# 400 pairs of row maxima beside the projections, and one exponential for two heads

## The chip, the cores and the metric

The kernel runs on one core of a Trainium2 chip, whose engines work side by side: TensorE (PE in the profile, its weight loads PEld), VectorE (DVE), ScalarE (ACT), GpSimd (POOL), and SyncE (SP), whose queue issues the transfers. The metric is the device time of one execution in microseconds (us).

## What is computed

Two transformer layers with the same weights over 2048 tokens of width 640. Each layer is

```python
x = x + attention(layernorm(x)) @ wo        # 32 heads of 20
h = relu(layernorm(x) @ w1 + b1)
x = x + (h * h) @ w2 + b2                   # 1536 hidden
```

where attention is `softmax(q k^T / sqrt(20)) v` over all 2048 keys, for every head. Most matrices are held as two parts, a high one and the rest, and multiplied in three products (high by high, high by rest, rest by high).

## The kernel before

**Heads and blocks.** Four heads form a group (8 groups); a block `t` is one group against one quarter `qb` of the queries (512 of them): 32 blocks a layer. In a group, head `2 * p + par` lies on the upper or lower 64 partitions by `par`, so a score product takes 60 rows there, or 62 with two more that carry the negated row maximum.

**Maxima.** The softmax subtracts each query's true maximum, which must be known before a block's scores are made. It is found by a product of its own the other way round: 128 queries by 512 keys (`by_queries`, L463), reduced along the keys on VectorE into a small tile `mx`. For each block there are 2 pairs of heads x 4 groups of 128 queries x 4 key quarters `c`, so 32 *pairs* (a pair: both `par`), 1024 a layer. They are found in three ways:

- `smax` (L475): one head, one bank, one reduction of 512; used inside attention.
- `smax_two` (L484): a pair on two banks, one reduction of 1024; used beside the projections.
- *doubles*: for two neighbouring key quarters at once. From the difference of the keys (`kd`, made beside the projections and stored in `d_kd`) `step_two` makes a pair of products and ScalarE's relu of them (L495); `both_two` makes the products with the first quarter, and VectorE adds the relu and takes the maximum (L505, with a short read of the accumulator). So one double stands for two plain pairs, with the same number of products and half the passes over them on VectorE.

**The projection stage** (`qkv`): 40 units of 15 products make q and k (L308), 16 of 30 make v (L355). `between` counts products, and at every `PACE` of them calls `some`, which puts maxima between: the end of a double begun in the last call, one plain pair, and the start of a double; three uses of two-bank pieces. These come in turn from banks 0 to 5 (`ps_q`). The lists `PLAIN` and `DOUBLE` say which blocks are ready at which unit; a plain item is `(group, qb, c)`, a double `(group, qb, "d")` for quarters 0 and 1, `"e"` for 2 and 3. After the doubles the rest is plain, three pairs per 11 products. `tiles` asks for the keys and queries of an item and of the one after it when the item begins.

**Attention** (`attention`): a written order of letters is walked, `a` and `b` a score and its exponential for the even or odd head of a pair (L560, L567), `m` and `n` one maximum for an even or odd head, `V` the weighted sum of a key tile of 128 keys (L572, four heads beside each other in bank 7, single precision in two passes). Each string holds eight key tiles; its key in `ORDERS` is the number of maxima pairs in it, which `pairs` chooses by what is due. Scores use banks 0 to 3 in turn (`ps_st`), maxima 4 to 6. Pairs already done beside the projections are left out of the list. At a block's end ScalarE copies the sums out of bank 7 (L585).

All instructions keep the order in which the program issues them, on each engine; semaphores alone tie the engines.

Of the kernel before, what the change touches and what calls it, by code (L numbers as in the profile page):

```python
# [16 lines left out]
P = 128  # L17
# [22 lines left out]
def tile_layers(  # L40
# [52 lines left out]
    ps_st = Ring(0, 1, 2, 3)  # L93
# [359 lines left out]
    def maxima(t):  # L453
        if t not in mx_t:
            mx_t[t] = small.tile([P, 4, 4, 4], F32, tag="mx", bufs=14, name=name("mx"))
            if t in PARTLY:
                nc.vector.memset(mx_t[t], LEAST)
        return mx_t[t]
# [92 lines left out]
    def score(t, kt, h, es):  # L551

        p, par = divmod(h, 2)
        if p not in es:
            es[p] = weights[len(e_n) % len(weights)]
            e_n.append(t)
        dst = ps_st("st")
        b = 64 * par
        assert t in done
        nc.tensor.matmul(  # L560
            dst,
            k_t[t // NQB, kt // 4][b : b + 62, p, (kt % 4) * P : (kt % 4 + 1) * P],
            q_t[t][b : b + 62, p, :],
            start=True,
            stop=True,
        )
        nc.scalar.activation(es[p][:, par, :], dst, AF.Exp, scale=SCALE)  # L567
# [72 lines left out]
    def prep_job():  # L640
# [7 lines left out]
        if jobs:  # L648
# [11 lines left out]
        ([], [(1, qb, c) for qb in (1, 2, 3) for c in (2, 3)]  # L660
         + [(2, qb, c) for qb in range(3) for c in range(NQB)]),
    ]
    DOUBLE = [
# [4 lines left out]
         [(1, 3, "d"), (1, 0, "e")]),  # L668
# [6 lines left out]
    PACE = 8.2  # L675
# [3 lines left out]
    def qkv(first, x_src, rest):  # L679
# [5 lines left out]
        state = {"pace": 0, "n": 0}  # L685
        early, late, later_rows = {}, {}, []
        coming = [y for x in DOUBLE for h in x for y in h if y[2] == "d"]
# [34 lines left out]
        def tiles(x):  # L722
            g, qb, c = x
            for c in [c] if c in range(4) else [c, 2 * "de".index(c)]:
                if (g, c) not in k_t:
                    if c in range(4):
                        load_k(g, c, g > 1)
                    else:
                        load_kd(g, c)
            if g * NQB + qb not in q_t:  # L730
                load_q(g * NQB + qb)

        def end_group(x):
            g, qb, c = x
            t = g * NQB + qb
            rest = groups + double + [w[0] for w in work + twos] + [w[0][0] for w in begun]
            if t == 0:
                left[t] -= 1 if c in range(4) else 2
                if left[t] == 0:
# [7 lines left out]
            for y in [y for y in k_t if y[0] == g < 2 and y not in use]:  # L747
                del k_t[y]
# [22 lines left out]
        def some():  # L771


            while later_rows:
                mrows_load(later_rows.pop())
            if not (begun or double or twos):
                for _ in range(3):
                    one()
                return
            if begun:  # L780
                w, r = begun.pop()
                (g, qb, x), p, sub = w
                t = g * NQB + qb
                both_two(t, p, sub, x, r)
                c = 2 * "de".index(x)
                done.update([(t, p, sub, c), (t, p, sub, c + 1)])
                if (p, sub) == PAIRS[-1]:
                    end_group(w[0])
            one()
            w = following(double, twos)  # L790
            if w:
                (g, qb, x), p, sub = w
                begun.append((w, step_two(g * NQB + qb, p, sub, x)))
            else:
# [12 lines left out]
        for n, (tb, pos) in enumerate(UNITS):  # L807
# [5 lines left out]
            if 1 < n < NQB * FIRST + 2:  # L813
# [8 lines left out]
                if step == 3:  # L822
                    double.extend(DOUBLE[b][0] + DOUBLE[b][1])
# [6 lines left out]
        for tt in range(NKT):  # L830
            later(v_unit(tt, lambda: between(0.65)))
# [6 lines left out]
            if tt == 12:  # L838
# [3 lines left out]
                load_q(1)  # L842
        w_v.drop()
# [3 lines left out]
        for y in [y for y in k_t if y[0] == 1]:  # L847
            del k_t[y]
        assert 0 in done

# [8 lines left out]
        12: "naambbmVanmbambVbmannabVnabnmabVabnmbanVbbmnanaVbmmbaanVbmbmnaaV",  # L859
    }  # L860

    def attention(first, x_src, first_rows):
# [27 lines left out]
        def begin(i):  # L890
# [14 lines left out]
            if t == 1 and u % 4 == 1:  # L905
                load_k(3, u // 4, True)
# [15 lines left out]
        def op(o):  # L922
            if o in "ab":
# [8 lines left out]
                score(i // NKT, i % NKT, 2 * p + par, es_of.setdefault(i, {}))  # L932
# [40 lines left out]
        def pairs():  # L973
# [7 lines left out]
            n = min(max(round(state["debt"]), 12), 16)  # L981
# [3 lines left out]
        for o in "abab":  # L985
# [226 lines left out]
```

## Time and profile before

| | us |
|---|---|
| time, median of 3 (lowest, highest) | 3765.41 (3762.61, 3766.22) |
| the profiled execution | 3764.07 |
| its span in the profile | 3762.3 |
| projection stage, layer one | up to 373 |
| attention, layer one | 373 to 1464 |
| attention, layer two | 2247 to 3337 |

A group line of the profile names source line, engine, operation, the tile written and those read, the shape and the count; then the engine's busy time in us, the mean ns of one, and the idle time just before these instructions with what ended it. Instructions of one engine overlap, so the busy time divided by the count is less than the mean. A line of the timeline gives the start and length in us of neighbouring instructions of one kind, with their count; its length runs to the end of the last. A line of the windows gives the stretch, its length, and busy time (count) of PE, PEld, DVE, ACT and POOL, then TensorE's granted clock, the share of the transfer engines' time, and GB/s.

### The profile page before, as it was taken

What the parts mean: (1) busy time and instruction counts of PE and PEld (TensorE: products, weight loads), DVE (VectorE), ACT (ScalarE), POOL (GpSimd) and SP (SyncE); (2) the same over time, 40 slices, a digit from 0 to 9 for tenths busy, and PEclk for the clock granted to TensorE, in tenths of its full rate; (3) what the DMA queues carried; (4) which work ended last, traced back from release to release, by engine and by line L of the source; (5) the groups of instructions that cost most, each with busy time, mean ns of one, the idle gap of its engine ahead of it and who ended that gap; (6) DMA issues with size and microseconds to landing.
All of it is one profiled execution on the core that took longest, in us unless ns stands there. A gap on an engine that the chain in (4) does not pass through costs nothing.

```text
span 3762.3 us, 64260 instructions
## 1 busy us (share of the span) xinstructions
PE 3704.9 (98%) x23572; PEld 2127.4 (57%) x23572; DVE 2757.8 (73%) x4726; ACT 2573.2 (68%) x4951; POOL 830.4 (22%) x921
## 2 busy tenths in 40 slices
PE   6999999999999999999999999999999999999999
PEld 4667344444444445989876774444444444368998
DVE  7788888888888882444457878888888888814443
ACT  2454999999999995121224449999999999941221
POOL 6540234321122211111154201211221112101110
PEclk9999999999999999999999999999999999999999
DMA  7563454432212125611255443222222111365111
GB/s 224 182 206 133 130 174 143 146 81 67 64 49 57 44 91 188 230 43 43 95 171 179 160 142 82 77 67 64 70 73 55 54 54 43 98 213 195 43 46 40
DMA packets 258282, 405.87 MB, mean 108 GB/s; under 512 B 67828, under 2 KB 114676, under 8 KB 257968
## 3 DMA queue, kind: packets, MB, share of 16 engines
q1 hardware_dynamic: 257424, 400.06, 33.9%
q8 instruction: 186, 3.05, 0.3%
q10 hardware_dynamic: 544, 1.71, 0.2%
q14 instruction: 128, 1.05, 0.1%
HBM read 264.82 MB, written 136.81 MB: 107 GB/s over the span
## 4 chain that ended last, share of the span: by engine, by line
PE 93%; DMA 2%; DVE 2%; POOL 1%; ACT 1%; SPq 0%; issue 0%; ACTq 0%; DVEq 0%; POOLq 0%
PE banks L572 27%; PE banks L297 20%; PE banks L560 20%; PE banks L463 15%; PE banks L308 6%; PE banks L355 3%; DMA k<-d_qk 1%; DMA q<-d_qk 0%; SPq L76 0%; PE banks L1042 0%; DMA d_qk<-ev 0%; DVE h L268 0%; DVE r L1066 0%; POOL xnT L282 0%; DVE mx L484 0%; DVE bst L255 0%
## 5 line engine op out<-in xcount | busy, mean ns | idle before, releaser
L567 ACT ACTIVATE e<-banks 128x512 f32<-128x512 f32 x4096 | 2110.8, 612 | 52.6 <-PE banks L560 2.2
L475 DVE TENSOR_REDUCE mx<-banks 128x1 f32<-128x512 f32 x2928 | 1841.5, 685 | 218.9 <-PE banks L463 137.5
L560 PE MATMUL banks<-q,k 62*128 62x512 f32 x4096 | 1162.7, 435 | 2.7 <-DVE mx L484 2.2
L463 PE MATMUL banks<-k,q 60*128 60x512 f32 x3744 | 1153.7, 436 | 10.9 <-DMA q<-d_qk 10.1
L572 PE MATMUL banks<-e,vg 128*32 128x512 f32 x8192 | 1093.0, 605 | 0.0
L560 PEld LDWEIGHTS banks<-q,k 62*128 62x128 f32 x4096 | 600.6, 185 | 709.7 <-ACT e L567 668.7
L463 PEld LDWEIGHTS banks<-k,q 60*128 60x128 f32 x3744 | 537.2, 185 | 331.8 <-DVE mx L475 204.0
L495 ACT ACTIVATE rl<-banks 128x512 f32<-128x512 f32 x352 | 191.6, 596 | 255.7 <-PE banks L463 255.5
L572 PEld LDWEIGHTS banks<-e,vg 128*32 128x32 f32 x8192 | 161.6, 108 | 354.6 <-issue 327.6
L297 PE MATMUL banks<-w,h 128*128 128x320 f32 x2304 | 352.6, 311 | 2.9 <-DVE h L268 2.7
L297 PEld LDWEIGHTS banks<-w,h 128*128 128x128 f32 x2304 | 340.6, 188 | 12.4 <-DVE h L268 6.9
L297 PE MATMUL banks<-xnT,w 128*128 128x512 f32 x1440 | 331.8, 391 | 0.0
L1065 ACT ACTIVATE r<-banks,b_t 128x512 f32<-128x512 f32 x96 | 66.1, 689 | 380.8 <-PE banks L297 379.2
L308 PE MATMUL banks<-xnT,wqk 128*128 128x512 f32 x1200 | 324.2, 414 | 1.6 <-POOL wqk L282 1.6
L505 DVE CUSTOM_DVE_ANT_0 rl<-banks,rl 128x512 f32<-128x512 f32 x352 | 229.2, 689 | 121.3 <-PE banks L463 116.2
L297 PEld LDWEIGHTS banks<-xnT,w 128*128 128x128 f32 x1440 | 270.7, 189 | 55.6
L484 DVE TENSOR_REDUCE mx<-banks 128x2 f32<-128x1024 f32 x232 | 279.6, 1221 | 24.9 <-PE banks L463 24.3
L308 PEld LDWEIGHTS banks<-xnT,wqk 128*128 128x128 f32 x1200 | 220.1, 193 | 87.2 <-issue 43.4
L279 POOL CAST mr<-nt 128x32 fp32r<-128x32 f32 x64 | 13.5, 211 | 966.2 <-DVE nt L531 966.2
L616 POOL TENSOR_TENSOR few<-few,minus_t 128x16 f32<-128x16 f32 x62 | 179.9, 2901 | 199.0 <-DMA few<-d_s 197.1
L1085 DVE TENSOR_TENSOR x<-banks,x 128x320 f32<-128x320 f32 x128 | 62.8, 491 | 200.7 <-PE banks L297 191.6
L627 POOL TENSOR_TENSOR o<-o 128x512 f32<-128x512 f32 x62 | 79.6, 1285 | 560.2 <-DMA o<-d_r 276.3
(73 smaller groups left out, 1991.6 us busy)
## 6 DMA issues: line engine op xcount, KB each, us to landing
q<-d_qk SPq DMA_DIRECT2D x756, 80.0 KB
d_qk<-ev SPq DMA_DIRECT2D x80, 512.0 KB
k<-d_qk SPq DMA_DIRECT2D x468, 80.0 KB
x<-d_x SPq DMA_DIRECT2D x96, 320.0 KB
d_o<-ot SPq DMA_DIRECT2D x248, 80.0 KB
ot<-d_o SPq DMA_DIRECT2D x38, 512.0 KB
d_v<-v SPq DMA_DIRECT2D x32, 512.0 KB
vg<-d_v SPq DMA_DIRECT2D x32, 512.0 KB
```

Source lines behind the costliest of these rows:

```text
L297: nc.tensor.matmul(dst, a, b, start=(n == 0), stop=(n == last))
L308: nc.tensor.matmul(dst, w_qk.piece(pos * 10 + hw * KD + k), xt_[tb][k][:, hx, :], start=(n == 0), stop=(n == 3 * KD - 1),)
L355: nc.tensor.matmul(dst[:, :HALF], xt_[tb][k][:, hx, i * P : (i + 1) * P], w_v.piece(k * 4 + hw * 2 + hf), start=(j == 0), stop=(j == 3 * K ...
L463: nc.tensor.matmul(dst, q_t[t][b : b + 60, p, sub * P : (sub + 1) * P], k_t[t // NQB, c][b : b + 60, p, :], start=True, stop=True,)
L475: nc.vector.tensor_reduce(maxima(t)[:, 2 * p + par, sub, c : c + 1], dst, axis=AX.X, op=ALU.max)
L484: nc.vector.tensor_reduce(maxima(t)[:, 2 * p : 2 * p + 2, sub, c], dst, axis=AX.X, op=ALU.max)
L495: nc.scalar.activation(res[par], dst[:, par, :], AF.Relu)
L505: nc.vector.tensor_tensor_reduce(out=r[par], in0=dst[:, par, :], in1=r[par], scale=1.0, scalar=LEAST, op0=ALU.add, op1=ALU.max, accum_out= ...
L560: nc.tensor.matmul(dst, k_t[t // NQB, kt // 4][b : b + 62, p, (kt % 4) * P : (kt % 4 + 1) * P], q_t[t][b : b + 62, p, :], start=True, stop ...
L567: nc.scalar.activation(es[p][:, par, :], dst, AF.Exp, scale=SCALE)
L572: nc.tensor.matmul(acc[32 * h : 32 * h + 32, :], v_t[t // NQB, kt // 8][:, kt % 8, 32 * h : 32 * h + 32], es[p][:, par, :], start=(kt == 0 ...
L616: nc.gpsimd.tensor_tensor(few, few, minus_t, op=ALU.pow)
```

## The change

It has two parts.

In the projection stage doubles are found for the first three groups, but for the first two key quarters of the first block of groups 0 and 1, which stay plain as before: 176 doubles a layer for 88. Together with the plain pairs 400 of the 1024 pairs lie there, 292 before; the last 16 belong to group 3. Once all doubles are ready (`few` is false), `some` ends all doubles that were begun and fills three places with starts of new ones, at most two, so that calls alternate between two ends and one start, and one end and two starts; the pace is then 5.4 products instead of 8.2. Keys of group 2 are loaded for the doubles alone and again in attention, those of group 3 are loaded during the v units and kept, and `mx` has 16 buffers for 14.

In attention the letter `A` stands for both heads of a pair: two products into two neighbouring banks and one exponential over 1024 elements. The order strings may now hold ten pairs per eight key tiles. The strings for 12 and more stay in the source; the built program uses those of 10 and 11.

```diff
-    ps_st = Ring(0, 1, 2, 3)
+        def two(self):
+            self.n += 2
+            b = self.order[(self.n - 1) % len(self.order)]
+            return banks[:, b : b + 2, :]
+
+    ps_st = Ring(3, 0, 1, 2)
...
-    def score(t, kt, h, es):
+    def score(t, kt, h, dst):
...
+    def soft_two(t, kt, p, es):
+
+        e = weights_for(t, p, es)
+        dst = ps_st.two()
+        for par in range(2):
+            score(t, kt, 2 * p + par, dst[:, par, :])
+        nc.scalar.activation(e, dst, AF.Exp, scale=SCALE)
...
-        ([], [(1, qb, c) for qb in (1, 2, 3) for c in (2, 3)]
-         + [(2, qb, c) for qb in range(3) for c in range(NQB)]),
+        ([], []),
     ]
+    LAST = [(3, qb, c) for qb in range(2) for c in range(NQB)]
...
         ([(0, 3, "d"), (0, 3, "e"), (0, 2, "e"), (0, 1, "e"), (0, 0, "e")],
-         [(1, 3, "d"), (1, 0, "e")]),
+         [(1, 3, "d")] + [(1, qb, "e") for qb in range(NQB)]
+         + [(2, qb, x) for qb in range(NQB) for x in "de"]),
...
-    PACE = 8.2
+    PACE = 5.4
...
-            if not (begun or double or twos):
-                for _ in range(3):
-                    one()
-                return
-            if begun:
-                w, r = begun.pop()
-                (g, qb, x), p, sub = w
+            room = 3
+            while begun:
+                (x, p, sub), r = begun.pop(0)
+                g, qb, h = x
                 t = g * NQB + qb
-                both_two(t, p, sub, x, r)
...
+                both_two(t, p, sub, h, r)
...
+                room -= 1
+            if state["few"]:
+                one()
+                room -= 1
+            for _ in range(min(room, 1 if state["few"] and (groups or work) else 2)):
+                w = following(double, twos)
+                if w:
+                    (g, qb, x), p, sub = w
+                    begun.append((w, step_two(g * NQB + qb, p, sub, x)))
+                    room -= 1
+            for _ in range(room):
                 one()
...
-            pace = PACE if double or twos or begun else 11
+            pace = (8.2 if state["few"] else PACE) if double or twos or begun else 11
...
                 if step == 3:
+                    state["few"] = b < 3
...
+            if tt == 1:
+                groups.extend(LAST)
...
+            if tt in (13, 14):
+                for c in range(2 * tt - 26, 2 * tt - 24):
+                    if (3, c) not in k_t:
+                        load_k(3, c, True)
...
+        11: "AnAmnVAnmAVnAmmAVAnmnAVAnmAVmAnmAVAnmAVAmnnAV",
+        10: "AnmAVAnmmAVAmnAVAmmnAVAnmAVAnmnAVAnmAVAnmnAV",
...
-                for h in (0, 1, 2, 3) if g else (0, 1, 2):
+                for h in (0, 1, 2, 3) if g else (0, 1):
...
-                load_k(3, u // 4, True)
+                load_k(2, u // 4, True)
...
+            if o == "A":
+                i, p = divmod(st_n[0], 2)
...
+                soft_two(i // NKT, i % NKT, p, es_of.setdefault(i, {}))
...
-            n = min(max(round(state["debt"]), 12), 16)
+            n = min(max(round(state["debt"]), 10), 16)
...
-        for o in "abab":
+        for o in "AA":
```

More of the change, by code (lines that the diff above doesn't have):

```diff
@@ L454, in maxima @@
         if t not in mx_t:
[L455 removed]
+            mx_t[t] = small.tile([P, 4, 4, 4], F32, tag="mx", bufs=16, name=name("mx"))
             if t in PARTLY:
@@ L566, in score, with weights_for, soft_one @@
         )
-        nc.scalar.activation(es[p][:, par, :], dst, AF.Exp, scale=SCALE)
+    def weights_for(t, p, es):
+        if p not in es:
+            es[p] = weights[len(e_n) % len(weights)]
+            e_n.append(t)
+        return es[p]
+    def soft_one(t, kt, h, es):
+        p, par = divmod(h, 2)
+        e = weights_for(t, p, es)
+        dst = ps_st("st")
+        score(t, kt, h, dst)
+        nc.scalar.activation(e[:, par, :], dst, AF.Exp, scale=SCALE)
+    def soft_two(t, kt, p, es):
+        e = weights_for(t, p, es)
+        dst = ps_st.two()
+        for par in range(2):
+            score(t, kt, 2 * p + par, dst[:, par, :])
+        nc.scalar.activation(e, dst, AF.Exp, scale=SCALE)
     def pv(acc, t, kt, es, heads=(3, 2, 1, 0)):
@@ L684, in qkv @@
         done.clear()
-        state = {"pace": 0, "n": 0}
+        state = {"pace": 0, "n": 0, "few": True}
         early, late, later_rows = {}, {}, []
-        coming = [y for x in DOUBLE for h in x for y in h if y[2] == "d"]
+        coming = [y for x in DOUBLE for h in x for y in h if y[2] == "d" and y[0] < 2]
         def at(when, n, f):
@@ L746, in end_group @@
             use |= {(h, 2 * "de".index(y)) for h, y in use if y not in range(4)}
-            for y in [y for y in k_t if y[0] == g < 2 and y not in use]:
+            for y in [y for y in k_t if y[0] == g < 3 and y not in use]:
                 del k_t[y]
@@ L846, in qkv @@
         load_v(0, 1)
-        for y in [y for y in k_t if y[0] == 1]:
+        for y in [y for y in k_t if y[0] in (1, 2)]:
             del k_t[y]
@@ L922, in op @@
         def op(o):
-            if o in "ab":
+            if o == "A":
+                i, p = divmod(st_n[0], 2)
+                assert st_n[0] == st_n[1]
+                if i >= last:
+                    return
+                st_n[:] = [st_n[0] + 1] * 2
+                if i > state["begun"]:
+                    state["begun"] = i
+                    begin(i)
+                soft_two(i // NKT, i % NKT, p, es_of.setdefault(i, {}))
+            elif o in "ab":
                 par = "ab".index(o)
```

19 lines of the change are left out of this document (5 added, 14 removed).

## The prediction

> **What bounds the kernel now.** I read the engines and the chain of waits first, then the busy time by stage, then single stretches of the timeline.
>
> ```profile
> PE 3704.9 (98%) x23572; PEld 2127.4 (57%) x23572; DVE 2757.8 (73%) x4726; ACT 2573.2 (68%) x4951; POOL 830.4 (22%) x921
> ...
> PE 93%; DMA 2%; DVE 2%; POOL 1%; ACT 1%; SPq 0%; issue 0%; ACTq 0%; DVEq 0%; POOLq 0%
> PE banks L572 27%; PE banks L297 20%; PE banks L560 20%; PE banks L463 15%; PE banks L308 6%; PE banks L355 3%; DMA k<-d_qk 1%; DMA q<-d_qk 0%; SPq L76 0%; PE banks L1042 0%; DMA d_qk<-ev 0%; DVE h L268 0%; DVE r L1066 0%; POOL xnT L282 0%; DVE mx L484 0%; DVE bst L255 0%
> ```
>
> TensorE carries 93% of the chain: weighted sums (L572), scores (L560), maxima (L463). A busy TensorE need not be a full one, so two stages are looked at closely (windows in us; each busy time with its count).
>
> ```profile
> 30.00:375.00 345.00, 329.04 (x1691) 231.79 (x1689) 266.52 (x517) 145.77 (x278) 133.01 (x161) 0.98 0.55 186
> 2281.00:3270.00 989.00, 989.00 (x6960) 398.30 (x6956) 883.94 (x1447) 966.17 (x1885) 188.62 (x172) 1.00 0.24 66
> ```
>
> The first is the projection stage of layer one, the second 29 attention blocks of layer two: 1885 ScalarE instructions are 29 x (64 exponentials + 1 copy). One block is 989 / 29 = 34.10, one key tile 34.10 / 16 = 2.131 us. TensorE's share of one tile:
>
> ```profile
> 805.35 0.50 PE L560 MATMUL banks<-q,k 62*128 62x512 f32 x1
> 805.35 0.73 PE L463 MATMUL banks<-k,q 60*128 60x512 f32 x2
> 805.69 0.71 PE L560 MATMUL banks<-q,k 62*128 62x512 f32 x3
> 806.16 0.40 PE L463 MATMUL banks<-k,q 60*128 60x512 f32 x1
> 806.49 1.07 PE L572 MATMUL banks<-e,vg 128*32 128x512 f32 x8
> 807.48 0.50 PE L560 MATMUL banks<-q,k 62*128 62x512 f32 x1
> ```
>
> Seven products of 60 or 62 rows start between 805.35 and 806.16. Even heads use the array's lower half of rows, odd heads the upper, and two of different halves start together. So the seven make four **slots**; from the second (805.69) to the fourth (806.16) is 0.47, or 0.235 us a slot. First to second is 0.34, last slot to weighted sum 0.33, that sum 0.99; with two slots of 0.235, 2.13 us. The sum of starts equals the tile: TensorE bounds attention. An odd number of maxima wastes half a slot.
>
> ScalarE comes close behind:
>
> ```profile
> L567 ACT ACTIVATE e<-banks 128x512 f32<-128x512 f32 x4096 | 2110.8, 612 | 52.6 <-PE banks L560 2.2
> 806.38 1.57 ACT L567 ACTIVATE e<-banks 128x512 f32<-128x512 f32 x3
> ```
>
> Three exponentials back to back take 1.57 and the last lasts 0.61, so they start (1.57 - 0.61) / 2 = 0.48 us apart. Four need 1.92 of the 2.131.
>
> **Attention after the change.** The order of the built kernel holds per layer 268 tiles with three maxima, 222 with two and 22 with none; before it is 488 with three and 24 with none. A three-tile keeps four slots; a two-tile has three, hence 2.131 - 0.235 = 1.896. That is 222 x 0.235 = **52 us less** per layer, if nothing else becomes late.
>
> The exponential of 1024 elements isn't in the trace. Above, it starts two at 0.48 each, 0.96; below, it saves the fixed part. The elements' price comes from two copies:
>
> ```profile
> L274 ACT COPY r<-banks 128x512 f32<-128x512 f32 x88 | 51.4, 589 | 88.6 <-PE banks L308 41.4 <-PE banks L385 40.3 <-POOL kd L279 4.0
> L364 ACT COPY v<-banks 128x320 f32<-128x320 f32 x64 | 27.5, 429 | 45.3 <-PE banks L355 41.8 <-DMA k<-d_qk 2.9
> ```
>
> (589 - 429) / 192 = 0.83 ns an element, 0.43 us for 512 more: 0.48 + 0.43 = 0.91 us. I take 0.91, as the rate is that of the same engine and bank. Two tiles (one of each kind) last 4.03 and need four: 3.64, at worst 3.84. Either hides behind TensorE. (The Trainium skill, "ScalarE: Activation LUTs", section on what ACT_TABLE_LOAD costs, gives 186 ns + 0.833 ns per element and an overlap of 93 ns: 1039 ns, one every 0.95, an estimate that leaves the sum as it is. Its 612 ns for 512 elements is the row's 612; the overlap here is 0.13.)
>
> The ring is coarser: a pair of banks is written again one tile later, when its whole exponential is done. In a two-tile the first pair starts at 0, its exponential 0.5 later (0.50 for the product in the rows above) and the second at 0.54 + 0.91 = 1.45, done near 2.5. The next tile, a three-tile, writes that pair at 1.90 + 0.34 + 2 x 0.235 = 2.71. Slack 0.2 us: no wait. The copy of a finished block (as long as L274's, 0.6) goes between two exponentials and costs up to 0.2 where it falls behind a two-tile: 16 x 0.2 = 3 us. Tiles without maxima were bound by ScalarE:
>
> ```profile
> 1445.43 1.07 PE L572 MATMUL banks<-e,vg 128*32 128x512 f32 x8
> 1446.43 1.03 PE L560 MATMUL banks<-q,k 62*128 62x512 f32 x4
> 1447.39 1.07 PE L572 MATMUL banks<-e,vg 128*32 128x512 f32 x8
> 1448.39 1.18 PE L560 MATMUL banks<-q,k 62*128 62x512 f32 x4
> 1449.50 0.64 PE L572 MATMUL banks<-e,vg 128*32 128x512 f32 x4
> ```
>
> Two of them take 1449.50 - 1445.43, 2.03 each; after, two exponentials, some 1.85: 22 x 0.18 = 4. Attention: -52 - 4 + 3 = **-53 us a layer**.
>
> **The projection stage after the change.** The 108 pairs come back here. Products for maxima stand in groups of three slots between projection products; in the built order the groups rise from 100 to 136 a layer (64 to 85 between the q and k units, 36 to 51 between the v units). What a group costs:
>
> ```profile
> 188.63 0.39 PE L308 MATMUL banks<-xnT,wqk 128*128 128x512 f32 x1
> 188.95 0.73 PE L463 MATMUL banks<-k,q 60*128 60x512 f32 x4
> 189.52 0.40 PE L463 MATMUL banks<-kd,q 60*128 60x512 f32 x2
> 189.84 2.12 PE L308 MATMUL banks<-xnT,wqk 128*128 128x512 f32 x8
> 191.89 0.74 PE L463 MATMUL banks<-k,q 60*128 60x512 f32 x4
> 190.41 1.32 PE L308 MATMUL banks<-xnT,wqk 128*128 128x512 f32 x5
> 266.80 0.74 PE L463 MATMUL banks<-k,q 60*128 60x512 f32 x4
> 267.37 0.39 PE L463 MATMUL banks<-kd,q 60*128 60x512 f32 x2
> 267.70 2.02 PE L355 MATMUL banks<-wv,xnT 128*128 128x320 f32 x12
> 269.65 0.51 PE L463 MATMUL banks<-k,q 60*128 60x512 f32 x2
> 268.10 1.18 PE L355 MATMUL banks<-wv,xnT 128*128 128x320 f32 x7
> ```
>
> Five projection products take 1.32 with a last one of 0.39: 0.23 each (0.147 for v, from seven in 1.18 with a last of 0.31). A group with eight lasts 191.89 - 188.95 = 2.94; less 8 x 0.2325, 1.08 us. With twelve v products 2.85 - 12 x 0.147 = 1.09. So 36 groups add 36 x 1.085 = **39 us a layer**. Three bare slots would be 0.70 and 25 us; the rest is the change between full and half arrays (188.63 to 188.95 going in, 189.52 to 189.84 coming out, 0.32 each). (The Trainium skill, "TensorEngine Tiling (Array Packing)", Key Properties, says that changing the tiling mode drains TensorE. It speaks against this change, and the rows agree: by slots alone 25, with the drain 39.)
>
> Now what the quicker pace meets. A "double" is a product with the key difference, two relus on ScalarE, a second product and two VectorE reductions that add and take the maximum. Before, a group held one double's end, one plain pair, one double's start, with 8.2 products between; after, it alternates, 5.4 apart: group A ends two doubles and starts one, group B ends one and starts two. Each group goes once round the three bank pairs. VectorE's pace:
>
> ```profile
> 189.58 0.69 DVE L505 CUSTOM_DVE_ANT_0 rl<-banks,rl 128x512 f32<-128x512 f32 x1 [0.48 <-issue]
> 190.20 0.08 DVE L505 DVE_READ_ACCUMULATOR2_ANT mx<- 128x1 f32 x1
> 190.20 0.69 DVE L505 CUSTOM_DVE_ANT_0 rl<-banks,rl 128x512 f32<-128x512 f32 x1
> 190.81 0.08 DVE L505 DVE_READ_ACCUMULATOR2_ANT mx<- 128x1 f32 x1
> 190.81 1.22 DVE L484 TENSOR_REDUCE mx<-banks 128x2 f32<-128x1024 f32 x1
> ```
>
> A reduction starts 189.58 - 188.95 = 0.63 after its group, the next ones 0.61 apart. A and B hold six, 3.7 us, against some 4.65 for two groups on TensorE (one is 5.4 x 0.2325 + 1.08 = 2.34, beside v 8.3 x 0.147 + 1.09 = 2.31), so VectorE is not the bound in sum. But A's four end at 0.63 + 3 x 0.61 + 0.69 = 3.15. The last reads the second bank pair, and B's second slot writes it, at 2.33 + 0.34 = 2.67 after A's start. TensorE stands 0.48 and the release besides; from product to reduction that hand-over takes 0.63 - 0.50 = 0.13, so between 0.48 and 0.61: I take 0.55. The projection products queue behind it; nothing hides that. (Before, the reduction of that pair begins 190.81 - 188.95 = 1.86 in and ends at 3.08; the next group's second slot comes at 2.94 + 0.34 = 3.28.) The next A comes at 4.65 + 0.55 = 5.2 and its third slot, 0.57 in, at 5.77. It writes where B's last relus read:
>
> ```profile
> 189.95 1.09 ACT L495 ACTIVATE rl<-banks 128x512 f32<-128x512 f32 x2 [1.79 <-PE banks L463]
> ```
>
> A relu starts 189.95 - 189.52 = 0.43 after its product, the next 0.49 later, and lasts 0.6. B's four, from its second slot at 3.22, end at 3.22 + 0.43 + 3 x 0.49 + 0.6 = 5.72: no wait, but no slack; a copy of 0.45 in between could make one. The built order has 54 groups of kind B a layer: 54 x 0.55 = **30 us a layer**; bounds 0 and, with such a copy in each cycle, 54.
>
> Not charged: eight more clears of maxima on VectorE, which is idle for 78 of the 345 us, and the moved loads of keys. Loads are asked for one set of eight doubles ahead. That was 8 x 2.94 = 23.5 us and is now 5.3 groups of 2.6, 14 us; the queue's pace:
>
> ```profile
> 259.14 5.30 SPq L76 DMA_DIRECT2D q<-d_qk  x12
> ```
>
> Twelve issues in 5.3: eighteen at a change of keys take 8, inside 14.
>
> **Sum.** Per layer -53 + 39 + 30 = +16, for two layers +31. The profiled execution took 3764.07 (span 3762.3 and 1.8 around it), 1.3 under the median of three. 3764 + 31 = **3795 us**.
>
> **Rivals.** 1. *No stall in the projection stage.* The second bank pair comes free before TensorE asks, for instance as each half is released by itself or ScalarE holds A back. Then 3764 + 2 x (-53 + 39) = 3736, faster. It decides at 0.26 us of stall a cycle, where 2 x 54 x 0.26 = 28 eats the gain. For it: VectorE's sum is below TensorE's; against: TensorE works in order and the fourth reduction can't end before 3.1. 0.18.
> 2. *The coarse ring in attention.* If the 1024 exponential takes over 1.01 us a start (4.03 / 4), or the slack of 0.2 is eaten, two-tiles run at 2.13 and the 2 x 52 are gone: 3899. Against: both bounds are below 1.01. 0.07.
> 3. *More waits beside the projections*: relus late, or key and query loads late at 18 changes of set a layer. 25 us a layer more: 3845. For it: no slack in the relus; against: the loads fit their lead. 0.14.
> 4. The forecast, 3775 to 3815: 0.58; other 0.03. That the change doesn't do what it says is excluded by the order's counts.
>
> **Range and chances.** 3738 to 3848 leaves out rival 2 and half of rival 1. A measurement here tells 0.2% (7.5 us) from no change. Faster 0.19, same 0.08 (the forecast's lower edge), slower 0.73.
>
> **What would show it.** Right: attention blocks of 32.1 to 32.4 us; pair exponentials of about 1.04 us; in the projection stage TensorE idle before kind B's second slot, put down to the reduction, 0.4 to 0.7 us some 54 times a layer; that stage 60 to 75 us longer. Wrong: blocks above 33 (rival 2), or a stage under 45 us longer (rival 1), or waits for loads (rival 3).

## The result, and the profile after

The changed kernel takes 3826.03 us (median of 4 runs, 3821.35 to 3828.15), the kernel before beside it 3765.29 (3762.61 to 3766.22): a ratio of 1.0155, 95% interval 1.0143 to 1.0168. It is slower, as forecast, and inside the range, but 31 us above the forecast time: the change is +61 us where +31 was forecast. The profiled execution took 3821.35, the lowest of the four, with a span of 3819.6, 57.3 more than before.

The first page of the profile after, engines and two groups:

```profile
PE 3745.8 (98%) x23572; PEld 2065.6 (54%) x23572; DVE 2555.4 (67%) x4870; ACT 2615.2 (68%) x3255; POOL 829.1 (22%) x921
...
L589 ACT ACTIVATE e<-banks 128x1024 f32<-128x1024 f32 x2048 | 1967.5, 1027 | 112.1 <-PE banks L561 94.1
```

TensorE runs the same 23572 products at the same 98%, in a longer span: the share of busy time tells nothing here. VectorE's 2757.8 us fell to 2555.4, and nothing came of it. The exponentials of 1024 elements take 1.027 us.

So the stages have to be timed one by one. The first exponential of each layer's attention, from the timeline of ScalarE in the kernel after:

```profile
445.64 3.77 ACT L589 ACTIVATE e<-banks 128x1024 f32<-128x1024 f32 x4 [0.22 <-PE banks L561]
449.61 1.94 ACT L589 ACTIVATE e<-banks 128x1024 f32<-128x1024 f32 x2 [0.19 <-PE banks L561]
...
2350.84 3.77 ACT L589 ACTIVATE e<-banks 128x1024 f32<-128x1024 f32 x4 [0.23 <-DMA k<-d_qk]
```

| from the first exponential to the last of each attention, us | before | after | difference |
|---|---|---|---|
| up to attention, layer one | 373.2 | 445.6 | +72.4 |
| attention, layer one | 1091.5 | 1055.7 | -35.8 |
| from there to attention, layer two | 781.9 | 849.5 | +67.6 |
| attention, layer two | 1090.2 | 1043.2 | -47.0 |

The sum is +57.2. Both halves of the trade are there: attention gives, the projection stage takes, and it takes more.

**Attention.** A three-tile and a two-tile of the kernel after, from the timeline of TensorE:

```profile
2602.78 0.50 PE L561 MATMUL banks<-q,k 62*128 62x512 f32 x2
2603.12 0.63 PE L468 MATMUL banks<-k,q 60*128 60x512 f32 x3
2603.49 0.50 PE L561 MATMUL banks<-q,k 62*128 62x512 f32 x2
2603.92 1.06 PE L594 MATMUL banks<-e,vg 128*32 128x512 f32 x8
2604.91 0.50 PE L561 MATMUL banks<-q,k 62*128 62x512 f32 x2
2605.26 0.40 PE L468 MATMUL banks<-k,q 60*128 60x512 f32 x2
2605.49 0.40 PE L561 MATMUL banks<-q,k 62*128 62x512 f32 x2
2605.82 1.06 PE L594 MATMUL banks<-e,vg 128*32 128x512 f32 x8
2606.82 0.50 PE L561 MATMUL banks<-q,k 62*128 62x512 f32 x2
```

2.13 us with three maxima, 1.91 with two: the slot between 2605.26 and 2605.49 is 0.23, and one of them is gone. Blocks with 40 single maxima last 32.42 us, with 42 32.90, against 34.10 before.

**The projection stage.** A group of kind B there, with VectorE's reductions of the group of kind A ahead of it, from the timeline of the kernel after (L510 is the reduction, L468 the products for maxima):

```profile
302.64 0.69 DVE L510 CUSTOM_DVE_ANT_0 rl<-banks,rl 128x512 f32<-128x512 f32 x1
...
303.04 0.50 PE L468 MATMUL banks<-k,q 60*128 60x512 f32 x2
...
303.25 0.69 DVE L510 CUSTOM_DVE_ANT_0 rl<-banks,rl 128x512 f32<-128x512 f32 x1
...
303.39 0.18 PEld L468 LDWEIGHTS banks<-kd,q 60*128 60x128 f32 x1 [0.17 <-DVE mx L510]
303.39 1.34 PE L468 MATMUL banks<-kd,q 60*128 60x512 f32 x4
...
304.00 0.29 PEld L468 LDWEIGHTS banks<-kd,q 60*128 60x128 f32 x3 [0.43 <-DVE mx L510]
```

The fourth reduction of kind A runs until 303.25 + 0.69 = 303.94; the weights for the second product of kind B's second slot go in at 304.00, where 303.39 was its turn. TensorE stands 0.6 us, as the prediction's working has it. From the start of the first product to that of the last a group of kind B lasts 1.23 us in layer one and 1.25 in layer two (means of 54), where a kind A lasts 0.59 and 0.58 (60). TensorE's waits for that reduction from 100 to 425 us, from the list of waits (us in total, times, longest):

```profile
PEld banks L468 <- DVE mx L510: 35.7, 103, 0.5
```

Before the change such a list (90 to 345 us) has no wait of TensorE's for a double's reduction, and few for that of a plain pair:

```profile
PEld banks L463 <- DVE mx L484: 4.0, 13, 0.4
```

**A loss that the forecast hadn't priced there.** In layer one's attention TensorE stands twice for a tile of v (timeline of TensorE, after):

```profile
597.39 1.94 PE L594 MATMUL banks<-e,vg 128*32 128x512 f32 x8 [2.18 <-DMA vg<-d_v]
...
735.43 1.94 PE L594 MATMUL banks<-e,vg 128*32 128x512 f32 x8 [5.88 <-DMA vg<-d_v]
```

These two blocks last 36.28 and 40.88 us where their like take 32.42: 3.9 + 8.5 = 12.3 us, in layer one alone. SyncE's queue in the kernel after shows how late the second is asked for:

```profile
718.97 0.32 SPq L76 DMA_DIRECT2D d_r<-few  x1
719.38 5.05 SPq L76 DMA_DIRECT2D q<-d_m  x8
724.47 2.87 SPq L76 DMA_DIRECT2D d_w<-w  x4
727.39 3.26 SPq L76 DMA_DIRECT2D o<-d_r  x4
730.70 0.42 SPq L76 DMA_DIRECT2D raw<-in_B_w_dram  x1
731.16 0.43 SPq L76 DMA_DIRECT2D vg<-d_v  x1
```

All of this is issued one after the other, the v tile last, while TensorE already stands. Whether that order is the cause is tried in runs 8 and 9.

### The profile page after: what moved, and what is told of

It is laid out like the page before. It is cut to its first block, busy times and chain, and to the rows that moved or that the text cites. A ratio compares the mean times of both kernels' runs of the same rounds, so it can differ in the third digit from the quotient of the medians.

```text
span 3819.6 us, 65394 instructions
## 1 busy us (share of the span) xinstructions
PE 3745.8 (98%) x23572; PEld 2065.6 (54%) x23572; DVE 2555.4 (67%) x4870; ACT 2615.2 (68%) x3255; POOL 829.1 (22%) x921
## 4 chain that ended last, share of the span: by engine, by line
PE 54%; DVE 3%; issue 1%; ACT 1%; POOL 0%; DMA 0%; SPq 0%; DVEq 0%; ACTq 0%; POOLq 0%
PE banks L302 20%; PE banks L594 13%; PE banks L561 9%; PE banks L468 7%; PE banks L313 3%; DVE rl L510 2%; PE banks L360 1%; ACT e L589 1%; PE banks L1087 0%; DVE h L273 0%; DVE r L1111 0%; ACT h L272 0%; ACT r L1110 0%; DVE mx L510 0%; DVE mx L489 0%
## 5 line engine op out<-in xcount | busy, mean ns | idle before, releaser
L589 ACT ACTIVATE e<-banks 128x1024 f32<-128x1024 f32 x2048 | 1967.5, 1027 | 112.1 <-PE banks L561 94.1
L480 DVE TENSOR_REDUCE mx<-banks 128x1 f32<-128x512 f32 x2496 | 1581.2, 684 | 410.6 <-PE banks L468 396.5
L561 PE MATMUL banks<-q,k 62*128 62x512 f32 x4096 | 1002.2, 463 | 6.8 <-ACT e L589 5.8
L561 PEld LDWEIGHTS banks<-q,k 62*128 62x128 f32 x4096 | 395.4, 183 | 983.9 <-ACT e L589 959.9
L468 PE MATMUL banks<-k,q 60*128 60x512 f32 x3392 | 729.7, 415 | 5.8 <-DMA q<-d_qk 3.0
L510 DVE CUSTOM_DVE_ANT_0 rl<-banks,rl 128x512 f32<-128x512 f32 x704 | 443.2, 687 | 200.8 <-PE banks L468 176.5
L500 ACT ACTIVATE rl<-banks 128x512 f32<-128x512 f32 x704 | 380.4, 599 | 226.7 <-PE banks L468 225.4
L468 PEld LDWEIGHTS banks<-k,q 60*128 60x128 f32 x3392 | 376.4, 187 | 173.3 <-issue 64.0
L313 PE MATMUL banks<-xnT,wqk 128*128 128x512 f32 x1200 | 338.1, 420 | 0.5 <-POOL wqk L287 0.5
L468 PE MATMUL banks<-kd,q 60*128 60x512 f32 x704 | 185.0, 436 | 15.8 <-DMA q<-d_qk 4.4
```

Of the source, the lines that this page charges most:

```text
L313: nc.tensor.matmul(dst, w_qk.piece(pos * 10 + hw * KD + k), xt_[tb][k][:, hx, :], start=(n == 0), stop=(n == 3 * KD - 1),)
L468: nc.tensor.matmul(dst, q_t[t][b : b + 60, p, sub * P : (sub + 1) * P], k_t[t // NQB, c][b : b + 60, p, :], start=True, stop=True,)
L480: nc.vector.tensor_reduce(maxima(t)[:, 2 * p + par, sub, c : c + 1], dst, axis=AX.X, op=ALU.max)
L500: nc.scalar.activation(res[par], dst[:, par, :], AF.Relu)
L510: nc.vector.tensor_tensor_reduce(out=r[par], in0=dst[:, par, :], in1=r[par], scale=1.0, scalar=LEAST, op0=ALU.add, op1=ALU.max, accum_out= ...
L561: nc.tensor.matmul(dst, k_t[t // NQB, kt // 4][b : b + 62, p, (kt % 4) * P : (kt % 4 + 1) * P], q_t[t][b : b + 62, p, :], start=True, stop ...
```

## The experiments

Ratios are to runs of the kernel before on the same chip, with 95% intervals. "Mean tile" is worked out from the exponentials' row in the stretch from 2500 to 3250 us of layer two's attention: two pair exponentials make a tile, or four single ones. The row before the change and the one after it:

```profile
L567 ACT ACTIVATE e<-banks 128x512 f32<-128x512 f32 x1407 | 725.9, 612 | 17.4
...
L589 ACT ACTIVATE e<-banks 128x1024 f32<-128x1024 f32 x736 | 707.3, 1027 | 35.1 <-PE banks L561 29.2 <-PE banks L468 5.3
```

Before, 1407 single ones give 750 x 4 / 1407 = 2.132 us a tile; after, 736 pairs give 750 x 2 / 736 = 2.038.

**1. The attention part alone.** All of the projection stage is as before (doubles, lists, pace); the pair exponential stays. Twelve pairs per eight tiles are then due, so the string is

```diff
+        12: "AnmmAVAnmnAV" * 4,
```

> Projections as before (100 groups a layer, pace 8.2); attention with one exponential for two heads, three maxima in every tile (12 pairs per eight key tiles). Slot theory: seven products still need four slots, so a block stays at 34.1 us (up to 0.2 more for the copy), only the two blocks without or with few maxima gain some us: 3758 to 3772, like before. Rival, that it is the shorter work of ScalarE that sped up attention: about 0.1 us off every tile, blocks near 32.4, about 3660.

Measured: 3815.71 us (3812.05 to 3817.29), ratio 1.0124 (1.0109 to 1.0140). The pair exponential by itself gains nothing, so it isn't ScalarE that bound attention; but a loss of 0.9 us a block was in neither theory. The groups and the waits from 2500 to 3250 us of this kernel, and TensorE's weight loads for maxima:

```profile
L589 ACT ACTIVATE e<-banks 128x1024 f32<-128x1024 f32 x686 | 665.9, 1024 | 76.9 <-PE banks L561 73.3 <-PE banks L468 1.4
```

```profile
PEld banks L468 <- DVE mx L480: 78.7, 340, 0.4
```

```profile
2602.31 0.19 PEld L468 LDWEIGHTS banks<-k,q 60*128 60x128 f32 x2
2602.78 0.18 PEld L468 LDWEIGHTS banks<-k,q 60*128 60x128 f32 x1 [0.27 <-DVE mx L480]
```

A mean tile of 2.187, and 340 waits in some 343 tiles: the third of three maxima in a row finds its bank still with VectorE, which reduces one in 0.68 us.

**2. The same with the maxima spread.** One maximum in each place that held one before the change:

```diff
-        12: "AnmmAVAnmnAV" * 4,
+        12: "AnmAmVAmnAnV" * 4,
```

> The pair exponentials and nothing else of the change, as in the run with the attention alone (3815.71, blocks of 35.0 us), but with the written order of twelve maxima spread: in each key tile one maximum in each slot that held one before the change. Theory, that the 0.9 us per block came from a maximum's bank that VectorE had not given back, and that the pair exponential itself is worth nothing: blocks of 34.1-34.2 us as before the change, 3765-3770. Rival, that one exponential over two banks holds them longer and costs by itself: blocks stay above 34.6, 3795-3815. Second rival, that it relieves TensorE after all: blocks below 33.8, under 3750.

Measured: 3778.18 us (3771.38 to 3781.93), ratio 1.0026 (1.0016 to 1.0036), 8 us above the theory's range.

```profile
L589 ACT ACTIVATE e<-banks 128x1024 f32<-128x1024 f32 x700 | 679.2, 1024 | 64.3 <-PE banks L561 62.5 <-PE banks L468 1.3
```

2.143 a tile, blocks of 34.3; the wait for VectorE's bank no longer stands among the stretch's waits. The theory holds for 0.7 of the 0.9 us. The other 0.2 a block, 4.7 us by layer two's attention (1094.9 for 1090.2), belongs to the pair exponential or to this order of letters; which of them, no run separates. Another 6.6 us lie ahead of layer one's attention (379.7 for 373.2 in the profiled execution), where this run edits nothing. The two runs together say that this exponential earns nothing by itself.

**3. The projection part alone.** `A` is written `ab` in the strings of 10 and 11, so each head has its own exponential; all else is as changed. (The program's string of 11 has `VmAnmAVmAnmAV` in its second half; the line under The change reads `VmAnmAVAnmAV` there, one `m` short.)

```diff
-        10: "AnmAVAnmmAVAmnAVAmmnAVAnmAVAnmnAVAnmAVAnmnAV",
+        10: "abnmabVabnmmabVabmnabVabmmnabVabnmabVabnmnabVabnmabVabnmnabV",
```

> Projections as changed; attention with ten and eleven pairs per eight key tiles but one exponential per head. Slot theory: two-tiles need three slots, 1.90 us, where four exponentials at 0.48 and a sixteenth of a copy take 1.95; so the tile is bound by ScalarE there and a block takes 32.6 to 33.2 instead of 32.4 to 32.9: 3835 to 3870. Rival, that the pair exponential gives the gain: blocks back at 34.1, about 3920. If one exponential per head costs nothing, 3826.

Measured: 3854.44 us, ratio 1.0227 (1.0212 to 1.0242), as expected.

```profile
L581 ACT ACTIVATE e<-banks 128x512 f32<-128x512 f32 x1449 | 732.9, 619 | 10.4
```

ScalarE is busy for 733 of 750 us, and a mean tile takes 2.070. With two-tiles ScalarE is near its limit, and there the pair exponential is worth 2.070 - 2.038 = 0.032 us a tile, 16 us a layer. So the two-tiles give 2.132 - 2.070 = 0.062 a tile without the pair exponential, and it adds half as much again; by itself, with three maxima in every tile, it gave nothing (runs 1 and 2).

**4. The second reduction cut short.** VectorE reads 64 columns instead of 512 for the second head of each double, which leaves out a part of the maxima.

```diff
+            w = 64 if par else QB
...
-                in0=dst[:, par, :],
+                in0=dst[:, par, :w],
```

> As changed, but the second of a double's two VectorE reductions runs over 64 of 512 columns, so part of the maxima is left out. Stall theory: the fourth reduction of a group of kind A then ends some 0.9 us earlier, before TensorE asks for the bank pair; the 0.65 us in each of 54 groups of kind B a layer go, 108 x 0.65 = 70 us: about 3756. Rival, that the longer stage is TensorE's own work and switching, or relus that come late: no change or under 15 us, 3811 to 3826.

Measured: 3772.64 us (3769.82 to 3781.14), ratio 1.0017 (1.0008 to 1.0026). Kind B is back at 0.58 us, and the list of waits has, from 100 to 425 us:

```profile
PEld banks L468 <- DVE mx L511: 10.8, 36, 0.4
...
PEld banks L468 <- ACT rl L500: 5.7, 26, 1.2
```

35.7 us fell to 10.8, and the relu that was "no wait, but no slack" now makes one, at kind A's third slot (0.65 us where it was 0.59). From one attention to the next 820.6 us pass, 38.6 more than before the change; up to layer one's attention 420.7, 47.6 more. It is not faster than before, and 53 us of the expected 70 are gained, in part because layer one's attention has more waits for v than in the changed kernel: 14.8 us for 8.1, in blocks of 39.6 and 45.4 us, which cost some 20 us for 12.3. So the stall is VectorE's. By the times it is worth (3826.03 - 3772.64) / 2 = 27 us a layer, by the stages 24.9 and 28.9.

**5. Another order inside kind A**: end, start, end in place of end, end, start, so that the reductions of the second end come later and into another bank pair.

```diff
+            if not state["few"] and ends == 2:
+                end()
+                room -= 2 if start() else 1
+                end()
```

> As changed, but a group of kind A ends a double, starts one, ends the other (instead of end, end, start), so the bank pair that VectorE reads last is the third and is asked for 0.23 us later by kind B. Stall theory: the wait shrinks by about 0.23 of 0.65 us, 108 x 0.23 = 25 us: about 3801. If the wait is for relus on ScalarE instead, it grows or stays: 3826 or more.

Measured: 3802.68 us, ratio 1.0094 (1.0077 to 1.0111), as expected; kind B lasts 0.90 us from first to last product, and the next projection product starts 0.42 after its last one, where 0.32 was usual.

**6. The same with uneven gaps**, seven products after a group with two ends and five after the others:

```diff
+            state["next"] = 7 if ends == 2 else 5
...
-            pace = (8.2 if state["few"] else PACE) if double or twos or begun else 11
+            pace = (8.2 if state["few"] else state["next"]) if double or twos or begun else 11
```

> The order end, start, end in the groups with two ends (which alone gave 3803 and a stall of 0.42 us), and besides it seven products of projection after such a group and five after the others, where the mean is about six in both cases. Theory, that the stall at kind B is VectorE still reducing kind A's and the gap decides it: kind B's body (first to last product) falls from 0.90 to 0.60-0.65 us, 0.25-0.3 us x 54 x 2, 27-32 us less than 3803, so about 3772-3776 as far as as many maxima are taken beside the projections; each maximum that is not taken there turns a two-tile into a three-tile, 0.24 us. Rival, that the stall only moves to kind A's third slot: its body grows from 0.59 by what kind B's loses, time within 5 us of 3803.

Measured: 3784.51 us (3779.26 to 3788.35), ratio 1.0041 (1.0025 to 1.0058). Kind B is at 0.59 and 0.58 us, so its stall is gone; kind A has grown to 0.82 and 0.76 (median 0.63), a part of what the rival said. From one attention to the next 821.9 us pass, 40.0 more than before, and up to layer one's attention 426.6, 53.4 more; but with the longer gaps a layer has 131 groups, not 136. TensorE waits for v nowhere in this run. The price is where it was expected: by the built order 192 two-tiles are left in a layer, not 222, and layer two's attention takes 1052.0 us, not 1043.2. Of all versions that compute everything with both parts of the change this is the fastest, and still slower than before.

**7. Gaps of 6.6 and 4.6**, with the second v tile asked for earlier (the edit of run 8):

```diff
-            state["next"] = 7 if ends == 2 else 5
+            state["next"] = 6.6 if ends == 2 else 4.6
```

> The order end, start, end with gaps of 6.6 and 4.6 products (7 and 5 gave 3784.51), so that 211 two-tiles in a layer's attention instead of 192 are left, and the second v tile asked for earlier. Theory, that each group beside the projections costs 1.09 us without a stall and gives back about six two-tiles at 0.24 us, and that the stall begins again as the gaps shrink: 19 x 0.235 x 2 = 9 us gained in attention, some 3 groups a layer x 1.09 x 2 = 6-7 us lost beside the projections, and 0.05-0.1 us of stall x 108 = 5-10 us: 3782-3793. Rival, that the stall at 7 and 5 is already the least there is and doesn't change with the gaps: 3778-3783. Second rival, that it comes back whole, as with even gaps (0.42 us a group): 3800.

Measured: 3809.06 us, ratio 1.0111 (1.0096 to 1.0126); no theory was right. Kind B stays at 0.60, kind A goes to 0.86 and 0.89. But TensorE's longest waits are others, in each layer's projection stage (the list of waits from 1491 to 2340 us, which holds that of layer two):

```profile
PE banks L468 <- DMA q<-d_qk: 19.4, 5, 10.7
```

With the shorter gaps a group reaches its queries 10.7 us before they have landed; with 7 and 5 the longest such wait was 4.0 there, and 4.5 in layer one. The loads set a pace of their own. That is a part of the loss: from one attention to the next 848.2 us pass, 26 more than in run 6, and the waits for queries are 19.4 us for 10.0. And with the earlier request one wait for v stands in layer one (a block of 38.8 us), where run 6 had none.

**8. The v tile asked for earlier:**

```diff
-            if u in (2, 10) and qb == NQB - 1 and g + 1 < NG:
-                load_v(g + 1, u // 8)
+            if u in (2, 3) and qb == NQB - 1 and g + 1 < NG:
+                load_v(g + 1, u - 2)
```

> The changed kernel with one edit: the second v tile of the next pair of heads is asked for one key tile after the first (step 3 of the last block) and not eight later (step 10). Theory, that TensorE stands twice in the first layer's attention because that load is late: the waits of 2.2 and 5.9 us at the weighted sum for vg and what follows them go, layer 1's attention falls from 1055.7 to about 1044 us (the second's is 1043.2), the time by about 12 us, 3826 to about 3814. Rival, that SyncE's queue as a whole is late and some other load then arrives too late instead: within 3 us of 3826, with the wait at another tile.

Measured: 3826.6 us, ratio 1.0152 (1.0130 to 1.0174), no change. The two waits are gone, and one has come at the next v tile, in a block of 38.7 us (list of waits, layer one's attention):

```profile
PE banks L594 <- DMA vg<-d_v: 4.4, 1, 4.4
```

That is the rival.

**9. The v tile on ScalarE's queue:**

```diff
-                load_v(g + 1, u // 8)
+                load_v(g + 1, u // 8, nc.scalar)
```

> The changed kernel with the v tiles of the next heads asked for on ScalarE's queue in attention, and not on SyncE's, where they stood behind some 22 transfers; all else is as changed. Theory, that the two waits in the first layer's attention (2.2 and 5.9 us at the weighted sum, with the restart behind them 3.9 and 8.4 us) come from SyncE's order of issue: both go, that attention takes 1044 to 1047 us in place of 1055.7, no other load is late in their place, 3826 to about 3815. Rival, that what is late is only moved once more (as with the earlier request on SyncE's queue, which left one wait of 6.3 us at the next v tile): attention 1050 or more, 3820-3826. Second rival, that ScalarE waits for the tile's room before it can issue, with exponentials behind it: a block of over 36 us, time above 3826.

Measured: 3848.63 us, ratio 1.0213 (1.0194 to 1.0232): the second rival. TensorE waits for v no more, but ScalarE stands behind its own request (list of ScalarE's waits, layer one's attention):

```profile
ACT e L589 <- DMA d_s<-o: 18.5, 1, 18.5
ACT e L589 <- DMA d_o<-ot: 13.5, 2, 7.8
```

Blocks of 52.9, 41.5 and 41.0 us. What ends these waits are stores out of other tiles. In the source v tiles and these (`o`, `ot`) are buffers of one arena (`slot`, L67); I read the waits as the room for the v tile not being free until the stores have left, so that SyncE's order alone was not the cause. No run tries it. Which transfer is the first to be late was not found.

**10. The third maximum behind the second score**, in the changed kernel:

```diff
-        10: "AnmAVAnmmAVAmnAVAmmnAVAnmAVAnmnAVAnmAVAnmnAV",
+        10: "AnmAVAnmAmVAmnAVAmnAmVAnmAVAnmAnVAnmAVAnmAnV",
```

> The changed kernel with one edit: in the blocks' written order, the key tiles with three products besides their own take the third maximum after the second score and not right behind the second maximum. Theory, that bunched maxima wait for VectorE to give a bank back and make the three-tiles 2.151 us where before's spread ones took 2.133: three-tiles come to 2.13, 0.02 us x about 268 x 2, 10 us less, 3816. Rival, that ScalarE's exponential over two banks leaves the three-tiles longer whatever the order: no change within 3 us, 3826.

Measured: 3904.83 us, ratio 1.0369 (1.0351 to 1.0387), the slowest of all: both theories fell. The whole gain of the two-tiles is gone:

```profile
L589 ACT ACTIVATE e<-banks 128x1024 f32<-128x1024 f32 x703 | 675.2, 1023 | 64.6 <-PE banks L561 58.7 <-PE banks L468 5.5
```

750 x 2 / 703 = 2.134 a tile, as before the change. A three-tile after a two-tile there, on ScalarE and on TensorE:

```profile
2603.39 3.84 ACT L589 ACTIVATE e<-banks 128x1024 f32<-128x1024 f32 x4 [0.42 <-PE banks L561]
```

```profile
2604.70 0.50 PE L561 MATMUL banks<-q,k 62*128 62x512 f32 x2
2605.03 0.40 PE L468 MATMUL banks<-k,q 60*128 60x512 f32 x2
2605.39 0.50 PE L561 MATMUL banks<-q,k 62*128 62x512 f32 x2
2605.73 0.40 PE L468 MATMUL banks<-k,q 60*128 60x512 f32 x1
```

The second scores come 0.36 after the maxima (0.23 is usual), the lone maximum 0.34 after them (0.24 is usual). The second of the four exponentials, which reads the last tile's second pair of banks, runs from 2604.32 to 2605.33; the weights for the scores that write this pair go in at 2605.38. This is the coarse ring. In the changed kernel the three-tile shown above has it too:

```profile
2602.41 2.92 ACT L589 ACTIVATE e<-banks 128x1024 f32<-128x1024 f32 x3
...
2603.48 0.19 PEld L561 LDWEIGHTS banks<-q,k 62*128 62x128 f32 x2 [0.17 <-ACT e L589]
```

The first of these exponentials ends at 2602.41 + 1.02 = 2603.43, and the weights for its pair go in 0.05 later, the least seen in layer two's attention. The tile loses nothing: its second score starts at 2603.59 (2603.49 + 0.50, less the 0.40 of one product), which is its turn by slots, 2603.12 + 2 x 0.235. So the slack was 0.1 us, not the 0.2 of the prediction, and moving one maximum behind the scores takes 0.235 away. The loss stands in the three-tiles alone: from 2420 to 3320 us of the changed kernel and 2458 to 3358 of this one, 2.15 became 2.33 on average, while the two-tiles kept 1.91 and 1.90.

**11. That order with single exponentials** (run 3's kernel with run 10's order):

> The single exponentials of the run with the projections alone (3854.44; blocks of 32.99 and 33.42 us, ScalarE's own pace), with the written order of the run with the maxima apart (3904.83; blocks of 34.2). Theory, that the pair exponential holds both banks of a pair of scores until it ends, 1.02 us after it starts, and that in the orders with the maxima apart the second pair of scores comes 0.24 us earlier than that allows: one exponential for each head gives the first bank back after 0.61 us, so the same order costs little here, blocks of 33.0 to 33.6 us, 3850-3875. Rival, that the order itself is what costs (VectorE's bank for the lone third maximum, or the row halves that then don't alternate), whatever the exponential: blocks of 34.2-34.8, 3895-3920.

Measured: 3884.71 us, ratio 1.0311 (1.0294 to 1.0328).

```profile
L581 ACT ACTIVATE e<-banks 128x512 f32<-128x512 f32 x1422 | 718.1, 616 | 23.8 <-PE banks L561 16.5
```

2.110 a tile, blocks of 33.7 and 33.9, just above what the theory gave and under what the rival did. The order costs 2.110 - 2.070 = 0.040 a tile with single exponentials, and 2.134 - 2.038 = 0.096 with pairs. But 2.070 is ScalarE's pace, which hides a part of what the order costs; against the 2.038 of the pairs it is 2.110 - 2.038 = 0.072. So the pair's longer hold on its banks is worth between 0.02 and 0.06 of the 0.096, and the rest is there with either exponential. In this run, too, the last score of a three-tile starts 0.05 after the exponential that held its bank has ended (the median of 233 tiles): with single exponentials, too, TensorE's scores wait for ScalarE there.

## Why the prediction was right, and what it missed

The sign and the mechanism of the two halves were right; the size of the change was twice the forecast, and the range was wide enough to hold it. Point by point:

- **A slot of 0.235 us per two-tile**: right. 0.23 in the rows above; attention was forecast at -53 a layer and gave -47.0 in layer two. The mean tile is 2.038 us where the forecast's mix, (268 x 2.131 + 222 x 1.896) / 490, is 2.025; 0.013 x 490 is 6 us. The three-tiles take 2.15 on average (2420 to 3320 us) for the 2.131 assumed, the two-tiles 1.91 for 1.896, and most of that lies at a block's copy: the first whole tile behind it lasts 2.28 (2.25 before the change) and the block's last one 2.19 (2.15 before), the others 2.13. The second scores of these slow tiles wait for the exponential that holds their banks; here the copy has put it back:

```profile
2613.30 0.59 ACT L607 COPY o<-banks 128x512 f32<-128x512 f32 x1
...
2615.80 0.19 PEld L561 LDWEIGHTS banks<-q,k 62*128 62x128 f32 x2 [0.32 <-ACT e L589]
```

  The forecast had charged 0.2 for the copy in every other block, 3 us; but each block of 40 or 42 maxima lasts 0.2 longer than 34.10 less 8 or 6 slots, and the longer kind (32.90) lies outside the 32.1 to 32.4 named as a sign. The other 3 us are the tiles without maxima: they were to fall from 2.03 to 1.85, a gain of 4, and take 2.03 on average in layer two (2.05 before), a gain of half a microsecond, as there too scores wait for the pair's exponential.
- **The pair exponential**: taken as one every 0.91 us; two in 1.94 with the last 1.02 long make 0.92. The Trainium skill, "ScalarE: Activation LUTs", section on what ACT_TABLE_LOAD costs, gave 0.95 by its overlap of 93 ns; the row, with 0.10 to 0.11, decides, and the difference changes nothing here.
- **The ring's slack of 0.2 us**: too generous. It was 0.1 in the three-tile shown and gone behind a copy and in the tiles without maxima; "no wait" holds for the other tiles alone. Run 10 took the rest away, so rival 2 was one string of letters off.
- **36 more groups at 1.085 us, 39 a layer**: about right, but no run measures it alone. Run 4, with kind B's stall gone, shows 47.6 in layer one and 38.6 in layer two, about 4 of each being the new waits in kind A (60 groups, 0.06 to 0.07 longer). Run 6 shows 53.4 and 40.0, but for 31 groups more, and with 9 to 13 us in longer groups of kind A.
- **The stall of 0.55 us in kind B, 30 a layer**: right in place and cause, a little low for one stall and a little high for the layer: 0.6 in the rows, 1.25 - 0.59 = 0.66 by the groups' means, while run 4 puts its worth at 27 us a layer. The two banks are released one by one, as rival 1 had it, and that saves nothing, because the second product of the slot waits for the second bank, and all behind it too. The stage was to grow by 69 and grew by 72.4 and 67.6.
- **The loads**: here the prediction fell short. It weighed them beside the projections and found that they fit; in attention it priced none. Rival 3 named late loads and a price, but put them in the wrong stage. In attention they cost 12.3 us, in layer one alone, and which transfer is the first to be late stays open (runs 8 and 9).

The 31 us missed are thus some 12 of waits for v, 11 for tiles a little longer (6 in layer two, 5 in layer one), 2 for the stages, and 5 by which the median lies above the profiled execution; the last one is rounding. In the sum as it stood, -53 was the term mis-sized: it measured -47.0 in layer two and, with the waits for v, -35.8 in layer one.

What would have made it pay: without the stall, and with layer two's attention, a layer is 39 - 47 = -8 us, 16 us in all, an estimate from the terms above. None of the versions reached it: what ends the stall (longer gaps, run 6) takes fewer maxima away from attention, and what takes more (run 7) meets the loads.

## What to carry to other kernels

Work that is moved between two stages, both bound by the same engine, is paid for at the other stage's price: here 1.09 us for a group that saves about six slots of 0.235 (52 us over 36 groups, 1.45 each), a margin of 0.36 that a stall of 0.6 in some groups undoes. Before you raise the pace of a stage, follow each buffer once round its ring at the new pace, with the latest of its readers: the sum of an engine's work may fit (3.7 of 4.65 us) and its fourth instruction still end after the next user's turn. And when one instruction takes two buffers, count when both come free: an order of work that cost nothing may cost all of the gain.

## What the runs showed of the hardware

These waits cost TensorE more than their length. The stretches around the shorter wait for v in the kernel after (the last columns are the granted clock, the transfers' share and GB/s):

```profile
595.00:597.30 2.30, 0.21 (x2) 0.00 (x0) 1.29 (x2) 1.79 (x2) 2.15 (x3) 1.00 0.77 206
597.30:599.30 2.00, 1.91 (x10) 0.25 (x10) 0.00 (x0) 0.00 (x0) 1.92 (x4) 0.53 0.28 61
599.30:601.00 1.70, 1.70 (x10) 1.12 (x7) 0.49 (x1) 0.85 (x1) 0.82 (x1) 0.55 0.52 142
601.00:605.00 4.00, 4.00 (x30) 1.52 (x29) 2.92 (x6) 3.51 (x5) 1.41 (x3) 1.00 0.67 196
```

After 2.18 us of waiting the granted clock was 0.53 and 0.55 for the next 3.7 us; the weighted sum took 1.94 us for 1.06, and the block lost 3.9, not 2.2. The Trainium skill, "TensorE: Matmul & The Clock Gate", Part 1, has the clock halved after an idle window of about 3.4 us; in this trace a shorter wait was enough. The stalls of 0.6 us beside the projections didn't do it: from 160 to 440 us of the same kernel the granted clock was 1.00.
